# Sparse attention with an MoE block: key rows turned round, zero fills dropped, and the whole issue order rewritten

## The chip, the cores and the metric

The kernel runs on one core of a Trainium2 chip. The metric is the device time of one launch in microseconds (us); the median of three runs before the change is 217.11 us (216.6 to 217.87). The engines are named as in the profile: PE (TensorE matmuls), PEld (its weight loads), DVE (VectorE), ACT (ScalarE), POOL (GpSimd, which here issues all loads) and SP (SyncE, which issues the stores and some moves inside the chip).

## The reference

Four batches, eight heads, 768 positions, head size 64. Each query attends to the keys less than 16 positions away and, beside them, to 24 summaries of blocks of 32 positions; the result of the eight heads goes through two dense layers.

```python
k_sum = k.reshape(B, H, nb, 32, D).max(axis=3)
v_sum = v.reshape(B, H, nb, 32, D).mean(axis=3)
scores_l = where(abs(i - j) < 16, q @ k.T / 8, -1e9)
scores_s = q @ k_sum.T / 8 + log(32)
a = softmax(concat([scores_l, scores_s]))
x = a @ concat([v, v_sum])             # (4*768, 512) after the heads are joined
h = x @ w_in                           # 512 -> 2048
g = h * clip(h + 3, 0, 6) / 6
out = g @ w_out                        # 2048 -> 512
```

Inputs and output are float32; the kernel computes in bf16 and accumulates in float32.

## The kernel before

Queries are cut into 12 tiles of 64 a head. For each tile the stationary operand of the score matmul is a group of 120 key rows out of 128 in `kaug`: 32 rows of the tile before, the tile's own 64 rows, and the 24 block maxima. The queries are shifted by 16 positions (`PAD`), so that a query tile's window lies within these 96 rows. `vaug` holds the values in the same three groups of partitions: 0:32 from the tile before (the "halo", tokens `h`), 32:96 own, 96:120 the block sums (tokens `u` and their spreading). The scores of a half batch go to the "S" PSUM buffers (two of them), ACT takes exponentials (`exp`, L521), DVE multiplies with a 0/1 mask (`masking`, L522), and PE multiplies with `vaug` (tokens `v`). DVE takes the reciprocal and scales (L606), and the result is transposed into `x`, by PE for batches 0 and 1 and by DVE and SP for batches 2 and 3.

The dense part runs over eight half batches (`s` 0 to 7) of 384 rows. First layer: tokens `F{s}x{ft}`, 16 of them a half batch, each four matmuls of 128x128 by 384 columns into one of **three** "h" PSUM banks (L667); then ACT makes `relu` (L671) and DVE the product (`gate`, L672), which frees the bank. Second layer: tokens `G{s}{ts}x0`, parts 0 to 3 of four matmuls each with 512 columns into the one "o" bank (L684), a copy to SBUF (part 4) and a store (part 5); the last group is cut into 256 and 128 columns. So a first-layer group can start only when the product of the third group before it is done.

Batch 0 is special: its queries and keys are loaded in another layout and transposed on PE (`k0` to `k3`, `q0` to `q3`), its attention is taken apart (tokens `v00` to `v03`, the own part and the summed part as separate matmuls, `values1a` and `values1b`). For the later batches DVE transposes keys (`turn`, L456) and for batches 2 and 3 queries too (L460), tokens `w{b}{p}`, one for each pair of heads.

Nothing is scheduled by a compiler. The string `ORDER` lists about a thousand tokens, and each engine issues its own in that order and waits on semaphores for its inputs; `:A` and `:D` choose ACT or DVE for a copy that either can do. Tokens that begin with `-`, `~`, `_` or `=` are fills: matmuls on constant data (`keep`, L778) that only keep PE busy, of 128, 512 and 64 columns each, and `=n` one of 64n columns. POOL's loads are in the same string: `K`, `Q`, `V` for the inputs, `I` for w_in, `O` for w_out.

Of the kernel before, what the change touches and what calls it, by code (L numbers as in the profile page):

```python
# [9 lines left out]
F32 = mybir.dt.float32  # L10
BF16 = mybir.dt.bfloat16
# [18 lines left out]
c.0 K00.0 c.7 c.17 c.6 c.8:A K01.0 c.10:D c.5 c.1 _40 -15 k0.0 k0.2:A c.18 ~1 =2 k1.0 K02.0 ~12 =3 k2.0 k3.0 c.15:D c.2 c.3  # L30
s000.0 k0.3:A c.13:D c.4 c.11:A k1.1 Q00.0 q0.0 k1.4 k0.1 c.20 k1.2:A Q01.0 ~2 =5 q1.0 k0.4 k1.3:D c.9:A c.14:A c.19 k2.3:A
q0.1:A s000.1 q0.2:A =1 s010.0 s010.1 k2.2:A k3.2:D k3.3:D k3.1 V00.0 h000.0:D h001.0:D k2.1 k2.4 s000.2 ~2 =5 v00.0 V01.0 u0.0
h010.0:D s020.0 c.16 s010.2 q1.2:A u0.3:D u0.1:D u0.4:D v01.0 v01.1 v01.2 v00.1 q1.1:A V02.0 h020.0:A h021.0:A h011.0:A v00.2
s020.1 v01.3 v00.3 V03.0 u1.0 u1.3:A h030.0:D s030.0 k3.4 ~2 s030.1 u1.4:D v01.4 h031.0:D Q0w0.0 Q0w1.0 v01.5:D Q0w2.0 =1 q3.0
q3.1:D q2.0 u1.1:A u1.2:D s020.2 v02.0 v02.1 v02.2 s021.0 v02.3 s030.2 v03.0 v03.1 q2.1:A v03.2 s011.0 v03.3 v00.4 v00.5:D
v02.4 s021.1 s011.1 s021.2 v03.4 v03.5:D s011.2 v02.5:A s031.0 s031.1 s001.0 s031.2 I2.0 F0x3.0 F0x3.1 F0x3.2 F0x3.3 F0x3.4
F0x3.5 I4.0 F0x6.0 F0x6.1 F0x6.2 F0x4.0 F0x4.1 F0x4.2 F0x4.3 v411.0 v411.1 F0x5.0 F0x4.4 F0x4.5 v411.2 s001.1 I8.0 u0.2:A
s001.2 F0x8.0 F0x8.1 F0x8.2 F0x5.1 I0.0 F0x5.2 F0x11.0 F0x1.0 F0x11.1 F0x11.2 F0x1.1 F0x1.2 F0x1.3 F0x1.4 F0x1.5 v410.0 v410.1
F0x7.0 F0x7.1 F0x7.2 v410.2 F0x10.0 F0x10.1 I12.0 F0x13.0 F0x13.1 F0x15.0 F0x15.1 F0x13.2 F0x10.2 v411.3 v411.4:D v410.3
v410.4:A F0x15.2 F0x14.0 F0x14.1 F0x14.2 F0x9.0 F0x9.1 F0x9.2 F0x0.0 F0x0.1 F0x2.0 F0x2.1 K13.0 K10.0 c.12:A F0x0.2 K12.0 K11.0  # L40
w10.0 Q1w1.0 F1x14.0 F1x14.1 F1x14.2 F1x4.0 F1x4.1 F1x4.2 F1x2.0 F1x2.1 F1x2.2 w10.1:D F0x2.2 F0x2.3 F0x2.4 F0x12.0 F0x12.1
F0x12.2 F1x8.0 F1x8.1 F1x8.2 F1x1.0 F1x1.1 F1x1.2 F0x0.3 F0x0.4 F0x0.5 F0x2.5 F1x9.0 F1x9.1 F1x9.2 F1x5.0 F1x5.1 F1x5.2 F1x15.0
F1x15.1 w11.0 w11.2 F1x15.2 w11.3:D Q1w4.0 Q1w2.0 Q1w0.0 w10.2 w10.3:D q6.0 q6.1:A q7.0 q7.1:A F1x7.0 F1x7.1 w11.1:A F1x7.2
F1x12.0 F1x12.1 F1x12.2 O0.0 G02x0.0 Q1w5.0 Q1w3.0 q4.0 q4.1:A q5.0 q5.1:A F1x6.0 F1x6.1 F1x6.2 O1.0 G02x0.1 s100.0 s100.1
s100.3 F1x3.0 w12.0 F1x11.0 F1x11.1 w13.0 w13.2 F1x3.1 F1x11.2 w12.2 w12.1:D O2.0 G02x0.2 s101.0 s101.1 O3.0 F1x10.0 G02x0.3
G02x0.4:A w13.3:D w13.1:A s101.3 F1x0.0 G00x0.0 G00x0.1 w12.3:D s100.2 s101.2 s100.4 V10.0 h100.0:D F1x10.1 h110.0:A F1x10.2
F1x3.2 s110.0 s110.1 s110.2 s101.4 s110.3 G00x0.2 G00x0.3 G00x0.4:A V12.0 u4.0 h130.0:D h120.0:A F1x0.1 u4.1:D u4.2:A u4.4:D
u4.3:D u4.5:D G02x0.5 G01x0.0 G01x0.1 G01x0.2 s110.4 F1x0.2 h111.0:A v100.0 v100.1 v100.2 h121.0:A v101.0 v101.1 v101.2 G01x0.3
G01x0.4:A K20.0 K21.0 K22.0 K30.0 K23.0 w21.0 F1x13.0 F1x13.1 F1x13.2 v100.3 v100.4:A w20.0 w21.3 G12x0.0 w21.2:A v101.3
# [54 lines left out]
class Plan:  # L104
# [29 lines left out]
    def issue(self, keep):  # L134
# [28 lines left out]
def kernel(  # L163
# [80 lines left out]
    def low(x):  # L244

        return (1 - x) * HQ
# [563 lines left out]
```

## Time and profile before

| | before |
|---|---|
| median of the runs | 217.11 us |
| span of the profiled execution | 214.9 us |
| PE busy | 208.8 us, 97% |
| DVE busy | 162.7 us, 76% |
| ACT busy | 135.9 us, 63% |
| POOL busy | 49.5 us, 23% |
| first matmul of the first layer | 24.17 us |
| start of the last copy, after the last matmul | 211.96 us |

The span is the profiled execution from its first to its last instruction; the runs' times hold 2.2 us more around it. Times in the views count from the span's start. "Busy" counts overlapping instructions of an engine once. The digits of part 2 of the page are busy tenths in 40 slices of 5.4 us. In a timeline a line is start, duration, engine, line of the code, operation, and in square brackets the idle time before it and what ended it.

### The profile page before, as it was taken

How to read it: one execution, taken by the hardware profiler on the slowest of the kernel's cores; microseconds unless marked ns; L12 is line 12 of the kernel's file. 1: busy time of each engine (PE TensorE's matmuls, PEld its weight loads, DVE VectorE, ACT ScalarE, POOL GpSimd, SP SyncE). 2: the span in 40 equal slices, each digit the busy share in tenths (PEclk: the TensorE clock that was granted, in tenths of full speed). 3: DMA queues.
4: the chain of work that ended last, by engine and by line, in shares of the span. 5: the costliest groups of instructions: out<-in, count | busy, mean ns of one | idle time of the engine just before them, and what ended most of it. 6: DMA issues, size and time to landing. Idle time of an engine off the chain costs nothing.

```text
span 214.9 us, 6125 instructions
## 1 busy us (share of the span) xinstructions
PE 208.8 (97%) x2564; PEld 119.7 (56%) x2564; DVE 162.7 (76%) x318; ACT 135.9 (63%) x264; POOL 49.5 (23%) x66
## 2 busy tenths in 40 slices
PE   7998999999999999999999999999999999999994
PEld 7566656555555565565555555555555555564443
DVE  6987999999899999898899889887865555550021
ACT  3987878887898988756578696566346355520110
POOL 7977358906643244000000000000000000000000
PEclk9999999999999999999999999999999999999999
DMA  5999999999999999930334234113314400113123
GB/s 75 159 155 189 203 188 170 190 203 162 206 160 187 181 135 151 108 146 11 38 37 143 28 37 110 49 21 39 70 19 81 78 0 3 49 49 122 52 80 139
DMA packets 91724, 22.68 MB, mean 106 GB/s; under 512 B 82224, under 2 KB 88752, under 8 KB 91696
## 3 DMA queue, kind: packets, MB, share of 16 engines
q0 software_dynamic: 62288, 14.41, 72.7%
q1 hardware_dynamic: 29264, 7.80, 15.4%
q8 instruction: 20, 0.33, 0.6%
q10 hardware_dynamic: 144, 0.07, 0.1%
q14 instruction: 8, 0.07, 0.1%
HBM read 28.82 MB, written 6.29 MB: 163 GB/s over the span
## 4 chain that ended last, share of the span: by engine, by line
PE 86%; POOL 5%; DMA 4%; DVE 1%; ACT 1%; issue 1%; POOLq 0%
PE h L667 38%; PE o L684 33%; PE h L684 5%; DMA qwide<-in_q_dram 4%; PE S L624 3%; PE S L513 3%; POOL vaug L344 2%; PE S L554 1%; ACT vaug L242 1%; POOL first L306 1%; PE S L637 1%; POOL qwide L326 1%; PE S L440 1%; PE S L667 1%; POOL first L313 1%; PE h L582 1%
## 5 line engine op out<-in xcount | busy, mean ns | idle before, releaser
L667 PE MATMUL h<-x,win 128*128 128x384 bf16 x500 | 91.1, 326 | 0.3 <-DVE g L672 0.3
L671 ACT ACTIVATE r<-h 128x384 f32<-128x384 f32 x125 | 58.7, 492 | 38.8 <-PE h L667 36.8
L672 DVE SCALAR_TENSOR_TENSOR g<-r,h 128x384 bf16<-128x384 f32 x125 | 65.7, 546 | 22.7 <-ACT r L671 20.1
L684 PE MATMUL o<-wout,g 128*128 128x512 bf16 x336 | 81.7, 379 | 0.0
L667 PEld LDWEIGHTS <-win 128*128 128x128 bf16 x512 | 48.7, 98 | 35.9 <-issue 0.5
L684 PEld LDWEIGHTS <-g 128*128 128x128 bf16 x416 | 38.7, 98 | 37.4 <-issue 0.3
L521 ACT ACTIVATE at<-S 120x768 bf16<-120x768 f32 x24 | 18.6, 811 | 5.5 <-PE S L513 5.4
L242 ACT COPY ot<-o 128x512 f32<-128x512 f32 x17 | 10.0, 586 | 15.4 <-PE o L684 14.2
L522 DVE TENSOR_TENSOR at<-at,mask 96x768 bf16<-96x768 bf16 x24 | 12.6, 549 | 2.0 <-ACT at L521 1.6
L606 DVE TENSOR_TENSOR xn<-S,rc 128x768 bf16<-128x768 f32 x14 | 13.3, 950 | 0.3
L242 DVE COPY ot<-h 128x512 f32<-128x512 f32 (+1 forms) x3 | 1.6, 555 | 14.3 <-PE h L684 14.3
L344 POOL DMA_DIRECT2D vaug<-in_v_dram x10 | 11.8, 1191 | 0.4 <-DMA first<-in_k_dram 0.2
L684 PE MATMUL h<-wout,g 128*128 128x128 bf16 (+2 forms) x80 | 11.4, 294 | 0.0
L468 DVE TENSOR_REDUCE red<-kaug 128x24 bf16<-128x768 bf16 x12 | 11.2, 942 | 0.1
L242 ACT COPY vaug<-vaug 32x640 bf16<-32x640 bf16 (+3 forms) x17 | 8.9, 574 | 0.8 <-DMA vaug<-in_v_dram 0.5
L242 ACT COPY vaug<-vs 24x1536 bf16<-24x1536 bf16 x6 | 8.8, 1468 | 0.6 <-DVE vs L242 0.5
L456 DVE STREAM_TRANSPOSE kaug<-kraw 128x768 bf16<-128x768 bf16 x8 | 8.1, 1020 | 0.3 <-PE S L513 0.3
L778 PE MATMUL o<-idle 128*128 128x64 bf16 (+2 forms) x70 | 7.0, 278 | 1.1 <-DVE idle L288 1.1
L334 POOL DMA_DIRECT2D kraw<-in_k_dram x8 | 5.9, 737 | 8.9 <-DVE kaug L456 7.3
L513 PEld LDWEIGHTS <-kaug 32*128 32x128 bf16 x576 | 5.3, 92 | 4.4 <-issue 3.6
L643 DVE STREAM_TRANSPOSE y<-xn 128x768 bf16<-128x768 bf16 x8 | 7.6, 964 | 0.2
L624 PEld LDWEIGHTS <-at 120*64 120x64 bf16 x336 | 6.2, 111 | 2.6 <-issue 1.5
(107 smaller groups left out, 183.6 us busy)
## 6 DMA issues: line engine op xcount, KB each, us to landing
out_dram<-ot SPq DMA_DIRECT2D x19, 256.0 KB, 2.3
vaug<-in_v_dram POOLq DMA_DIRECT2D x6, 384.0 KB, 13.1
wout<-in_moe_w_out_dram POOLq DMA_DIRECT2D x4, 512.0 KB, 9.9
win<-in_moe_w_in_dram POOLq DMA_DIRECT2D x3, 512.0 KB, 10.8
kraw<-in_k_dram POOLq DMA_DIRECT2D x8, 192.0 KB, 12.9
x<-y SPq DMA_DIRECT2D x64, 24.0 KB, 2.0
first<-in_k_dram POOLq DMA_DIRECT2D x6, 192.0 KB, 12.3
first<-in_q_dram POOLq DMA_DIRECT2D x6, 192.0 KB, 12.3
```

Of the source, the lines that this page charges most:

```text
L242: {"ACT": nc.scalar.copy, "DVE": nc.vector.tensor_copy, "POOL": nc.gpsimd.tensor_copy}[eng](o, i)
L344: op("POOL", "dma128", lambda: nc.gpsimd.dma_start(out=o[BLK:WIN, a:z, 0:D], in_=rows[:, a:z]), w=[("v", b % 2, c) for c in range(lo, hi)] ...
L468: op("DVE", "max", lambda: nc.vector.tensor_reduce(red.slot[:], w[:, :, BLK:WIN].rearrange("p t (n c) -> p t n c", n=2), axis=AX.X, op=ALU ...
L513: nc.tensor.matmul(X[g // 2].slot[:, g % 2, i * QB:(i + 1) * QB], kaug[2 * u + m][rows, t], qT[rows, 2 * u + m, t * QB:(t + 1) * QB], star ...
L521: op("ACT", "exp", lambda a=a, e=e: nc.scalar.activation(a, X[e].slot[0:KEYS, :, 0:HALF], AF.Exp, scale=scl), r=[X[e]], w=[("at", p, half)])
L522: op("DVE", "masking", lambda m=m: nc.vector.tensor_tensor(m, m, mask[:, low(half):low(half) + HQ].unsqueeze(1).to_broadcast([WIN, 2, HQ, ...
L606: nc.vector.tensor_tensor(o, src[..., 0:D], r.unsqueeze(len(r.shape)).to_broadcast(list(o.shape)), op=ALU.mult)
L624: nc.tensor.matmul(X.slot[64 * c:64 * c + 64, i, m:m + D + 1], a[:, t * QB:(t + 1) * QB], vaug[b % 2][0:KEYS, h, t, 0:D + 1], start=True, ...
L667: nc.tensor.matmul(bank(h)[:, 0:HALF], w_in_sb[:, kt, cols], xt[s].slot[:, kt], start=(kt == 0), stop=(kt == NP - 1))
L671: op("ACT", "relu", lambda: nc.scalar.activation(r.slot[:], bank(h)[:, 0:HALF], AF.Relu, bias=0.5, scale=1.0 / 6.0), r=[h], w=[r])
L672: op("DVE", "gate", lambda: nc.vector.scalar_tensor_tensor(gt[s].slot[:, ft], r.slot[:], 1.0, bank(h)[:, 0:HALF], op0=ALU.min, op1=ALU.mul ...
L684: nc.tensor.matmul(o.slot[:, a:z], gt[s].slot[:, ft, ts * 128:(ts + 1) * 128], w_out_sb[:, ft, a:z], start=(ft == 0), stop=(ft == NFT - 1))
```

## The change

- **Key rows.** A tile's group becomes its own 64 rows first and the next 32 rows behind them; the 16 positions of shift lie at the other side. `qT`, `kaug`, `vaug`, the mask, the halo copies, the loads and the stores follow; half 0 of a batch is now tiles 0 to 5 and no longer 6 to 11.
- **No zero fills.** The block sums of v (`sums2`, `sums4`) read the own 64 rows alone, at partitions 0:64, and so need neither zeros in the halo rows (`empty`, eight operations, five on ACT and three on DVE) nor wait for them; a halo copy no longer waits until the sums are taken.
- **Block sums by 128 queries.** For batch 0, `values1b` multiplies two query tiles at once: 6 matmuls for a pair of heads and no longer 12.
- **Fills.** `idle` becomes a bf16 view of a float32 tile of ones, and a new fill token `^n` issues n products of float32 by float32 with 512 columns. The fills before: `_40 -15 ~1 =2 ~12 =3 ~2 =5 =1 ~2 =5 ~2 =1`. After: `_36 -16 ^3 ~2 ^1 =6 ~1 =3`.
- **Order.** The string is new throughout. The loads of batch 0 and of w_in keep their places in POOL's order (but for the three `Q0w`); behind them the loads are permuted. Some copies change engine.

```diff
-c.0 K00.0 c.7 c.17 c.6 c.8:A K01.0 c.10:D c.5 c.1 _40 -15 k0.0 k0.2:A c.18 ~1 =2 k1.0 K02.0 ~12 =3 k2.0 k3.0 c.15:D c.2 c.3
+c.0 K00.0 c.11 K01.0 c.1 c.7 c.8 K02.0 _36 -16 k1.0 c.2 c.3 c.6 k1.1 k0.0 k1.4 c.10 c.9 Q00.0 c.5 Q01.0 V00.0 ^3 ~2 q0.0 k2.0
...
+v03.1 v03.2 v01.5:A ~1 =3 q3.0 v03.3 q2.0 Q1w4.0 q3.1:D v00.4 s021.0 u1.2:D v00.5:D q2.1:A v02.4 v02.5:D s031.0 v03.4 s021.1
+F0x3.0 u1.4:D F0x3.1 s031.1 v03.5:D F0x3.2 s011.0 s031.2 F0x3.3 s001.0 F0x6.0 s011.1 s021.2 F0x4.0 F0x4.1 F0x3.4 s011.2 F0x3.5
...
+s100.0 K20.0 F1x12.2 F1x10.1 s100.3 F1x10.2 w12.0 s100.1 G02x0.2 F1x5.0 w13.2 G02x0.3 w13.1:D w12.1:A s101.0 G02x0.4:A s101.3
+F1x0.0 w12.2 K31.0 G00x0.0 G00x0.1 s101.1 w13.3:A w12.3:D s110.0 V22.0 G00x0.2 G00x0.3 F1x5.1 F1x13.1 Q32.0 s110.1 F1x5.2
+s100.2 s101.2 s100.4 s110.3 s110.2 K30.0 h130.0:D u4.0 G00x0.4:A Q22.0 F1x13.2 G01x0.0 F1x0.1 G01x0.1 s110.4 u4.1:D G01x0.2
...
+G32x0.1 v211.2 w31.4:A G32x0.2 F4x9.2 u6.2:A v211.3 v210.3 G32x0.3 F4x2.1 v211.4 F4x2.2 G32x0.4:A w33.0 F4x14.0 u6.4:D G11x0.5
+F4x13.0 F4x14.1 v211.5 F4x13.1 F4x7.0 v211.6 w30.4:A G30x0.0 F4x14.2 F4x7.1 F4x13.2 G30x0.1 F4x7.2 w32.3 F4x6.0 w32.4:A w33.3
...
-G70x0.4:D G70x0.5 G60x0.0 G60x0.1 G60x0.2 G72x0.4:D G72x0.5 G60x0.3 G71x256.1 G71x256.2 G60x0.4:D G60x0.5 G71x256.3 G71x256.4
-G71x384.0 G71x384.1 G71x384.2 G71x384.3 G71x384.4:D G71x384.5
+G60x0.4:A G72x0.3 G70x0.1 G71x0.4:D G50x0.5 G71x384.0 G61x0.5 G71x384.1 G71x384.2 G72x0.4:A G70x0.2 G71x256.0 G71x384.3 G70x0.3
+G71x0.5 G71x256.1 G70x0.4:A G72x0.5 G71x256.2 G71x384.4:D G60x0.5 G71x384.5 G71x256.3 G71x256.4 G70x0.5
...
-    ind = sb([WIN, NQ, 32], BF16, "ind")
+    ind = sb([QB, NQ, 32], BF16, "ind")
-    idle = sb([128, 128], BF16, "idle")
+    ones = sb([128, 128], F32, "ones")
+    idle = ones[:].bitcast(BF16)[:, 0:128]
...
     def low(x):
-        return (1 - x) * HQ
+        return x * HQ
...
-    def empty(eng, i, c):
-        o = vaug[i][0:BLK, 2 * c:2 * c + 2, :, 0:D].bitcast(F32)
-        if eng == "DVE":
-            nc.vector.memset(o, 0.0)
-        else:
-            nc.scalar.activation(o, idle[0:BLK, 0:1].unsqueeze(1).unsqueeze(1).to_broadcast([BLK, 2, NQ, D // 2]), AF.Copy, scale=0.0)
...
-        op("POOL", "dma128", lambda: nc.gpsimd.dma_start(out=o[BLK:WIN, a:z, 0:D], in_=rows[:, a:z]),
+        op("POOL", "dma128", lambda: nc.gpsimd.dma_start(out=o[0:QB, a:z, 0:D], in_=rows[:, a:z]),
...
+        def summed():
+            for T in range(3):
+                for h in range(2):
+                    nc.tensor.matmul(bank(X)[:, part(T, h)], at[p][WIN:KEYS, h, 2 * T * QB:(2 * T + 2) * QB], vf[p][WIN:KEYS, h, 0:D + 1],
+                                     start=False, stop=T == 2 and h == 1)
...
     def keep(n, m, o):
-        n, c = (1, n) if m == 3 else (n, (2, 8, 1)[m])
+        n, c = (1, n) if m == 3 else (n, (2, 8, 1, 0, 8)[m])
+        w = ones[:] if m == 4 else idle
         for _ in range(n):
-            nc.tensor.matmul(o[:, 0:c * 64].rearrange("p (c x) -> p c x", c=c), idle[:], idle[:, 0:64].unsqueeze(1).to_broadcast([128, c, 64]),
+            nc.tensor.matmul(o[:, 0:c * 64].rearrange("p (c x) -> p c x", c=c), w, w[:, 0:64].unsqueeze(1).to_broadcast([128, c, 64]),
                              start=True, stop=True)
```

211 lines of the change are left out of this document (100 added, 111 removed).

## The prediction

> **What bounds the kernel now.** I read the page first, whose digits by slice ask for the busy time by stage, then who PE waited for, then PE's timeline at the start.
>
> ```profile
> 24.17:58.30 34.13, 33.81 (x511) 19.63 (x506) 31.68 (x61) 27.99 (x52) 20.05 (x23) 1.00 1.75 187
> 58.30:123.90 65.60, 65.50 (x848) 36.66 (x849) 60.56 (x105) 50.59 (x99) 10.66 (x12) 1.00 1.12 111
> 123.90:211.95 88.05, 88.02 (x765) 48.18 (x763) 50.47 (x92) 39.31 (x81) 0.00 (x0) 1.00 0.24 56
> 211.95:214.90 2.95, 0.00 (x0) 0.00 (x0) 0.29 (x1) 0.00 (x0) 0.00 (x0) 1.00 0.39 133
> sum 214.90, PE 208.84 PEld 119.68 DVE 162.67 ACT 135.95 POOL 49.46; mean PE 41.77 PEld 23.94 DVE 32.53 ACT 27.19 POOL 9.89
> ```
>
> A row is a stretch, its length, then the busy time of PE, PEld, DVE, ACT and POOL, the granted clock (1.00), DMA. PE is busy 208.8 of 214.9 us and without a gap from 24.17 on, so the time is PE's work plus what it spends on fills and waits. DVE's total, 162.7, is 76%, but that is a mean: from 58.3 to 123.9, which is from the block sums of batch 1 (`u4.0`) to the middle of F4, it has 60.56 of 65.60, 92%, and behind that 57%.
>
> ```profile
> PE h L667 <- DVE g L672: 0.3, 1, 0.3
> ```
> ```profile
> 1.13 3.71 PE L778 MATMUL o<-idle 128*128 128x64 bf16 x55 [1.13 <-DVE idle L288]
> ...
> 5.99 0.53 PE L392 MATMUL h<-ident,first 96*64 96x96 bf16 x16 [0.26 <-DMA first<-in_k_dram]
> 6.45 2.85 PE L778 MATMUL o<-idle 128*128 128x512 bf16 x13
> ...
> 20.31 0.73 PE L442 MATMUL h<-ident,qwide 128*128 128x128 bf16 x10 [0.81 <-DMA qwide<-in_q_dram]
> ...
> 21.28 0.38 PE L582 MATMUL h<-vf,at 24*64 24x65 bf16 x12
> 21.59 0.35 PE L490 MATMUL S<-qT,kaug 64*128 64x64 bf16 x12
> ...
> 24.17 2.12 PE L667 MATMUL h<-x,win 128*128 128x384 bf16 x12
> ```
>
> Of the first 24 us about nine are fills; the stage's last wait ends when the last piece of q lands, just ahead of 20.31. From 24.17, where the first layer starts, to 211.96, where the last copy starts, PE waits only once, 0.3 us for a gate on DVE. So a gain must come from an earlier 24.17, and everything behind it must keep pace with PE; DVE, with 5 us to spare in the stretch of 65.6, is the one to watch.
>
> **The change part by part.** *The start.* The loads up to w_in keep their places, so the last q still lands at 20.3 (three loads of the same bytes only change places). What changes is how much is behind that landing. Before, the matmuls, reciprocals and scales of v02 and v03 came after it; now they come before it. From the landing I count for the new order: q3 and q2 0.73 (21.04), v00's transpose 0.2, then s021 waits for the copy of q3, which stands on DVE behind v03's scale (a copy 0.56, so about 21.6), two score groups at 0.31 (21.28 to 21.59 is one group of twelve), and two transposes at 0.2: first layer at 22.7 in place of 24.17, a gain of 1.47. Without any wait it is 22.2; with DVE half a us later, 23.2. But two score groups that stood before 24.17 (s011, s001) now stand behind: 0.62 back. Against that, PE changes from small matmuls to F or G 26 times behind this point and no longer 28 times, at 0.11 each (below): 0.2. Sum -1.47 + 0.62 - 0.2 = **-1.05**, with ends -0.5 and -1.5.
>
> *Zero fills, sums by 128 queries, fills by float32.* Six matmuls less for each of four pairs are 4 x 0.15 = 0.6 us of PE, but all stand ahead of 20.3, where PE waits 0.81 for q now: nothing, and -0.6 if q came earlier. The eight zero fills stand almost all ahead of the first keys' landing (the matmul at 5.99 waits for DMA): nothing. The three float32 products stand between the first two key groups (the second ends at about 6.9) and the first q, which POOL issues at 4.75 and which lands 5.2 later, at 9.9:
>
> ```profile
> first<-in_q_dram POOLq DMA_DIRECT2D x1, 192.0 KB, 5.2
> ```
>
> They have 3 us. No row shows a float32 product: a bf16 one of 512 columns is 0.22 (thirteen in 2.85, the last one short); if each operand is worked on as two halves it is four times that, 0.87, and three with two bf16 ones take 3.0. I take 0.87; from 0.22 to 0.87 they cost nothing, and if the clock is low in them too (the row of 55 fills makes 4480 columns in 3.71 us, half the rate of the thirteen) they take 5.1 and end near 12.5, 2.6 us late for q, of which PE's slack ahead of 20.3 (0.7 us, counted on its work from q to the landing) and a fill behind them leave some 1.5. The Trainium skill, FP8 and Floating Point Precision, section TensorE Precision Notes, says that true float32 takes four passes. By that rule the three take 2.6 us, as above; no run here shows it yet.
>
> *The order in the middle.* F4x7 takes the bank that F4x2's gate frees. Take PE from the end of `u4.0` to F4x7's start in the new order, and DVE from `u4.1` to F4x2's gate, which is all that it must do by then. The prices are from these rows:
>
> ```profile
> 55.19 0.48 PE S L513 x48
> ...
> 57.50 0.84 PE S L554 x48
> ...
> 61.09 0.95 PE S L624 x48
> 62.03 0.97 PE o L684 x4
> ...
> 65.19 1.73 PE o L684 x8
> 66.91 1.30 PE h L667 x8
> ```
> ```profile
> 28.92 1.48 DVE L672 SCALAR_TENSOR_TENSOR g<-r,h 128x384 bf16<-128x384 f32 x3
> ```
> ```profile
> L606 DVE TENSOR_TENSOR xn<-S,rc 128x768 bf16<-128x768 f32 x14 | 13.3, 950 | 0.3
> L522 DVE TENSOR_TENSOR at<-at,mask 96x768 bf16<-96x768 bf16 x24 | 12.6, 549 | 2.0 <-ACT at L521 1.6
> L468 DVE TENSOR_REDUCE red<-kaug 128x24 bf16<-128x768 bf16 x12 | 11.2, 942 | 0.1
> L456 DVE STREAM_TRANSPOSE kaug<-kraw 128x768 bf16<-128x768 bf16 x8 | 8.1, 1020 | 0.3 <-PE S L513 0.3
> L643 DVE STREAM_TRANSPOSE y<-xn 128x768 bf16<-128x768 bf16 x8 | 7.6, 964 | 0.2
> L242 DVE COPY vaug<-vs 24x1536 bf16<-24x1536 bf16 x6 | 3.4, 573 | 0.2
> L599 DVE RECIPROCAL rc<-S 128x12 f32<-128x12 f32 x14 | 3.0, 222 | 0.2
> ```
> ```profile
> L521 ACT ACTIVATE at<-S 120x768 bf16<-120x768 f32 x24 | 18.6, 811 | 5.5 <-PE S L513 5.4
> ```
>
> PE: 37 F at 0.65 (24.05), 32 G at 0.863 (27.6), eight values at 0.47, five scores at 0.48, two sums at 0.78, four transposes at 0.34 (11.1 together), and twelve changes back to F or G at 0.11 (0.97 less 0.86): **62.1 us**. DVE: an instruction in a row costs some 0.03 less than its mean, as three gates in 1.48 and not 1.64 show. 36 gates at 0.494 (17.8), eleven masks at 0.52 (5.7), eight reciprocals and scales at 1.12 (9.0), fourteen transposes of keys and queries at 0.99 (13.8), six maxima at 0.91 (5.5), six spreads at 0.54 (3.2), four block transposes at 0.93 (3.7), and thirteen small copies, 3.5 in all: **62.2 us**. So the new order asks DVE for all of its time in this stretch. The old order has 39 F and 35 G between the same two points, 65.7 us of PE, for about the same work of DVE; the new one has two F and three G fewer there, and puts a query transpose, two halo copies, two copies of x, three small ones of q and an output copy more on DVE. And DVE does not start level. The gate of F1x5 stands behind its relu, which on ACT's order stands behind the two exponentials of s101 (0.81 each), a copy of G02 (0.56) and one of keys (0.41): 2.9 us after s101 on PE. Behind that gate are another gate, five masks and a halo copy, 3.9 with it; so `u4.1` can start 6.9 us or more after s101 ends, while PE needs 5.6 (one F, four G, s110 and the sums) to the end of `u4.0`. That is 1.3; the relu before s101's has 0.3 more in front. I take 1.6, in place of 0.1 now, with 0.8 as the low end. F4x7 then starts 1.6 + 62.2 + 0.05 - 62.1 = **1.75 us** late, and PE has waited that much by then, in steps: the same sum to F3x15 (84 instructions against 49.9 us of PE) gives 1.0. Bounds: if `u4.1` starts level, and DVE's prices are 1% lower, nothing; with every mean at its full row (0.546 a gate), it would be over 4, which the row of three gates excludes; I hold 0 to 2.6. Behind 123.9 DVE's share falls to 57%, and it falls behind no more.
>
> *Loads in the middle.* The pieces of w_in still land as before, and F now needs them a us earlier: 0.1, at most 0.4. The later loads need no more than now: the first need of each stands about where it stood, behind as many bytes.
>
> *The end.* The old order ends with a 128-column piece: a copy of 0.29, a 64 KB store.
>
> ```profile
> 211.96 0.29 DVE L242 COPY ot<-h 128x128 f32<-128x128 f32 x1 [0.82 <-PE h L684]
> ```
> ```profile
> out_dram<-ot SPq DMA_DIRECT2D x1, 64.0 KB, 1.6
> ```
> ```profile
> out_dram<-ot ACTq DMA_DIRECT2D x1, 64.0 KB, 2.1
> ```
> ```profile
> out_dram<-ot SPq DMA_DIRECT2D x19, 256.0 KB, 2.3
> ```
>
> Copy and store take 0.3 + 1.6 = 1.9, and the span ends 1.05 after. The new one ends with a 64 KB store by ACT (0.33 + 2.1) and, beside it, a whole 256 KB one whose copy ends as PE does (2.3 to 2.5): 2.4, so **+0.5** (0.3 to 0.7).
>
> Sum: -1.05 + 1.75 + 0.1 + 0.5 = +1.3 on 214.9, a span of 216.2. The median of the runs is 217.11; the 2.2 around the span stay. The 0.1 of w_in is left out, because PE waits longer for DVE later anyway: 217.11 + 1.2 = **218.3 us**.
>
> **The rivals.** *DVE keeps up.* Everything hangs on 1.6 us of start and on 1% of 62; if DVE's small copies are cheaper or the exponentials of s101 come sooner, the middle costs nothing: -1.05 + 0.1 + 0.5 = -0.45, **216.6**, no change that shows. For it: the old order left PE one wait. Against it: 92% became 100%. It isn't slower, and it decides once `u4.1` starts within 0.1 us of `u4.0`'s end. *The start gives all and the end costs nothing:* -1.5 at the start, middle and end nothing: **215.6**. The copy of 256 KB would have to land in 2.0. *The fills cost:* PE is left idle from the end of the 52 fills (4352 columns, to about 4.7) until the second key piece, the one that the matmul at 5.99 waits for, and the float32 products run at the low rate: 1.5 later, **219.5** or more. The Trainium skill, TensorE: Matmul & The Clock Gate, section What's actually happening, has the clock fall only after an idle window of about 3.4 us, so not by these 1.3 us; the longest idle time here, 0.81, shows no fall, and no run shows 1.3.
>
> **How the numbers follow.** A measurement here can't tell under 0.5%, 1.09 us, from no change: faster is below 216.0, slower above 218.2. My forecast has 0.55 and, with its spread of 0.6, lies above 218.2 in 0.35 and between in 0.20. DVE keeps up: 0.27, of which 0.17 between and 0.10 below. The full gain: 0.08, below. The fills: 0.10, above. Faster 0.18, same 0.37, slower 0.45. The range reaches from the full gain to the fills, 215.8 to 219.5; the forecast's own is 217.5 to 219.1.
>
> **What would show it.** The first F matmul at 22.2 to 23.2, with the last q landing at 20.3. PE waiting for DVE's gates (L667 behind g L672) and for scales between 75 and 130 us, together 1 to 2.5 us, and DVE at 98% or more of 60 to 120. The float32 fills at 0.87 each, ending before 10 us. 3.4 us or more from the last matmul's end to the span's end. I am wrong if PE's waits behind 45 us stay under 0.5 us, or if the first F comes after 23.5.

## The result, and the profile after

The changed kernel takes 220.0 us (median of 219.11 to 221.57) against 216.86 (216.36 to 217.87): a ratio of 1.015, 95% interval 1.0101 to 1.0199. It is slower by 1.5%; 218.3 was predicted, and at most 219.5. Here and below the ratio and its interval leave out executions that are more than 1.5% above the fastest of the same kernel, and the medians count all. The profiled execution has a span of 217.8 us against 214.9; its own time is 219.55.

First the busy time by stage, cut where the prediction cut it (PE, PEld, DVE, ACT, POOL, granted clock, DMA).

```profile
24.69:58.30 33.61, 32.68 (x478) 19.33 (x481) 30.72 (x59) 27.09 (x56) 17.99 (x23) 1.00 1.79 183
58.30:123.90 65.60, 64.05 (x878) 36.21 (x886) 62.71 (x112) 47.11 (x96) 12.52 (x13) 1.00 1.06 104
123.90:213.95 90.05, 89.21 (x763) 49.09 (x773) 49.34 (x96) 40.74 (x80) 0.00 (x0) 1.00 0.27 62
213.95:217.80 3.85, 0.22 (x4) 0.04 (x1) 0.00 (x0) 0.44 (x2) 0.00 (x0) 0.92 0.29 101
```

The first F (the first matmul of the first layer) comes at 24.69 in place of 24.17, from there to the start of the last matmul it takes 189.26 in place of 187.53, and the end from there 3.81 in place of 3.18: +0.5, +1.7 and +0.6. DVE's work from 58.3 to 123.9 is 62.71 of 65.60 us, 96%, where it was 60.56.

PE's timeline of the start, and then DVE's:

```profile
6.33 0.87 PE L383 MATMUL h<-ident,first 96*64 96x96 bf16 x32 [1.39 <-DMA first<-in_k_dram]
7.13 3.27 PE L775 MATMUL o<-ones 128*128 128x512 f32 x8
...
15.90 0.83 PE L527 MATMUL h<-vaug,ind 64*32 64x128 bf16 x23 [1.04 <-DMA vaug<-in_v_dram]
...
23.68 0.35 PE L481 MATMUL S<-qT,kaug 64*128 64x64 bf16 x12 [0.76 <-DVE qT L242]
...
24.69 0.65 PE L663 MATMUL h<-x,win 128*128 128x384 bf16 x3
```
```profile
12.74 0.96 DVE L394 TENSOR_REDUCE red<-h 128x24 bf16<-128x768 bf16 x1 [1.41 <-ACT kaug L242]
...
22.60 0.56 DVE L602 TENSOR_TENSOR xn<-h,rc 128x384 bf16<-128x384 f32 x1
23.08 0.55 DVE L242 COPY qT<-S 128x768 bf16<-128x768 bf16 x1
```

The last piece of q landed at 20.13, and yet the copy of q3, which I had ending at 21.6, starts at 23.08 and ends at 23.63. DVE has no idle time from 12.74 on: 10.3 us of its work stand between the third pair's maximum (`k2.1`) and that copy. The last idle time ahead of them is the 1.41 us in which the maximum waits for ACT's copy out of the same PSUM bank (`k2.3`).

Behind the first F, PE's waits, the moves on SP and ACT at the end:

```profile
PE o L680 <- issue: 1.2, 4, 0.7
...
PE h L663 <- DMA x<-y: 0.7, 1, 0.7
```
```profile
102.21 11.09 SPq L645 DMA_DIRECT2D x<-y  x16
```
```profile
214.86 0.27 ACT L694 COPY ot<-h 128x128 f32<-128x128 f32 x1 [0.74 <-DMA out_dram<-ot]
215.16 0.37 ACTq L695 DMA_DIRECT2D out_dram<-ot  x1
```

PE never waits for a gate. It waits 0.7 us at 57 for nothing that the profile shows ("issue"), 0.7 at 116 for the sixteen moves of x to F4 (0.69 us each to issue), and the last piece waits for an output buffer, that is for an older store to land. In the second profile of this kernel (`e18`) nothing shows at 57, the same F4 group waits 0.93 us at 117, which the profile puts down to DVE, and the last piece does not wait; from the first F to the end both take 193.1 us.

### The profile page after: what moved, and what is told of

The parts are those of the page before. It is cut to its first block, busy times and chain, and to the rows that moved or that the text cites. A ratio compares the mean times of both kernels' runs of the same rounds, so it can differ in the third digit from the quotient of the medians.

```text
span 217.8 us, 6018 instructions
## 1 busy us (share of the span) xinstructions
PE 206.1 (95%) x2498; PEld 119.1 (55%) x2525; DVE 159.5 (73%) x316; ACT 129.5 (59%) x257; POOL 49.4 (23%) x66
## 4 chain that ended last, share of the span: by engine, by line
PE 76%; DVE 6%; DMA 6%; SPq 4%; issue 3%; POOL 1%; ACT 1%; DVEq 0%; ACTq 0%; POOLq 0%
PE h L663 36%; PE o L680 29%; SPq L645 4%; PE h L680 3%; DMA first<-in_q_dram 3%; PE S L504 2%; DVE vaug L242 2%; PE S L620 2%; DMA out_dram<-ot 2%; DMA x<-y 1%; POOL first L296 1%; PE S L633 1%; PE S L663 1%; DVE red L394 1%; DVE xn L602 1%
## 5 line engine op out<-in xcount | busy, mean ns | idle before, releaser
L663 PE MATMUL h<-x,win 128*128 128x384 bf16 x500 | 93.3, 326 | 0.7 <-DMA x<-y 0.7
L667 ACT ACTIVATE r<-h 128x384 f32<-128x384 f32 x125 | 59.6, 492 | 44.2 <-PE h L663 43.1
L680 PE MATMUL o<-wout,g 128*128 128x512 bf16 x311 | 78.6, 379 | 2.4 <-issue 1.2
L335 POOL DMA_DIRECT2D vaug<-in_v_dram x10 | 12.2, 1229 | 13.0 <-DVE rc L595 11.5
L513 DVE TENSOR_TENSOR at<-at,mask 96x768 bf16<-96x768 bf16 x24 | 12.7, 546 | 1.9 <-ACT at L512 1.9
L459 DVE TENSOR_REDUCE red<-kaug 128x24 bf16<-128x768 bf16 x12 | 11.1, 934 | 0.0
L242 ACT COPY kaug<-h 128x576 bf16<-128x576 bf16 (+3 forms) x12 | 4.1, 413 | 7.2 <-DVE red L394 7.0
L775 PE MATMUL o<-ones 128*128 128x64 bf16 (+3 forms) x60 | 7.1, 302 | 1.1 <-DVE ones L280 1.1
L242 DVE COPY ot<-h 128x256 f32<-128x256 f32 (+1 forms) x2 | 0.7, 358 | 10.0 <-PE h L680 10.0
L242 ACT COPY vaug<-vs 24x1536 bf16<-24x1536 bf16 x5 | 7.3, 1468 | 0.2
## 6 DMA issues: line engine op xcount, KB each, us to landing
wout<-in_moe_w_out_dram POOLq DMA_DIRECT2D x4, 512.0 KB, 10.3
kraw<-in_k_dram POOLq DMA_DIRECT2D x8, 192.0 KB, 10.4
first<-in_k_dram POOLq DMA_DIRECT2D x6, 192.0 KB, 13.5
first<-in_q_dram POOLq DMA_DIRECT2D x6, 192.0 KB, 10.3
```

The source lines that it names most:

```text
L242: {"ACT": nc.scalar.copy, "DVE": nc.vector.tensor_copy, "POOL": nc.gpsimd.tensor_copy}[eng](o, i)
L335: op("POOL", "dma128", lambda: nc.gpsimd.dma_start(out=o[0:QB, a:z, 0:D], in_=rows[:, a:z]), w=[("v", b % 2, c) for c in range(lo, hi)], s ...
L459: op("DVE", "max", lambda: nc.vector.tensor_reduce(red.slot[:], w[:, :, 0:QB].rearrange("p t (n c) -> p t n c", n=2), axis=AX.X, op=ALU.ma ...
L513: op("DVE", "masking", lambda m=m: nc.vector.tensor_tensor(m, m, mask[:, low(half):low(half) + HQ].unsqueeze(1).to_broadcast([WIN, 2, HQ, ...
L663: nc.tensor.matmul(bank(h)[:, 0:HALF], w_in_sb[:, kt, cols], xt[s].slot[:, kt], start=(kt == 0), stop=(kt == NP - 1))
L667: op("ACT", "relu", lambda: nc.scalar.activation(r.slot[:], bank(h)[:, 0:HALF], AF.Relu, bias=0.5, scale=1.0 / 6.0), r=[h], w=[r])
```

## The experiments

Ratios are to the kernel before, timed on the same chip. All kernels but the twelfth and the fifteenth are made from the changed one.

### Is it the order or the layout?

**Old order, new layout** (`e1`):

```diff
-(the new ORDER)
+(the ORDER of before: no empty(), load pieces renamed)
```


> The changed kernel with the order of before: its layout, its dropped zero fills, its block sums over 128 queries, but the old order and the old bf16 fills. If the new order is what costs (my theory: about 0.9 us at the start, 1.4 in the middle, 0.65 at the end), this one is as fast as before or a little faster: ratio 0.995 to 1.001, first F matmul at 23.9 to 24.2, no wait of PE above 0.5 us behind it. If the layout costs (rows of v in partitions 0 to 63 land later, as the trace of after shows 1.2 to 1.9 us later than before), V00 lands at about 14.4 here too, the first F is at 24.7 or later and the ratio is 1.003 to 1.008.

217.53 us, ratio 1.0019 (0.9996 to 1.0042), just above what I expected. The layout, the dropped zero fills and the sums over 128 queries together cost 0.4 us, between nothing and 0.9; the order, with its fills, costs the rest of the 1.5%. From the first F to the end it takes 190.5 us, as before (190.7). But in its profile the first F comes at 25.47, and 24.7 or later was my sign that the layout costs. DVE's last idle time there is a wait for a piece of v:

```profile
14.82 1.01 DVE L242 COPY vaug<-vaug 32x768 bf16<-32x768 bf16 x3 [1.54 <-DMA vaug<-in_v_dram]
```

In the two profiles of before that wait is 0.67 and 0.86 us. So a part of what the start loses, up to 0.9 us, can be the layout's.

**Its counterpart** (`e9`): the old order up to the first F, the new one behind.

```diff
-c.0 K00.0 c.11 ... v03.4 s021.1 | F0x3.0 u1.4:D ...    (new | new)
+c.0 K00.0 c.7  ... s001.0 s031.2 | F0x3.0 F0x3.1 ...   (old | new)
```


> The counterpart of the fifth experiment: the changed kernel with the old order up to the first F matmul (as in the first experiment) and the new order behind it. If start and rest add up as the two traces of before and after say (rest 193.1 us from the first F to the end, less 0.6 for the two score groups that now stand ahead, against 190.5 with the old rest), this kernel takes 1.5 to 2 us more than the first experiment: 218.9 to 219.6, ratio 1.010 to 1.014. If the start alone carries the loss (fifth experiment: new start and old rest give 1.0158, as slow as after), it is as fast as the first: 1.001 to 1.004.

219.76, ratio 1.0119 (1.0078 to 1.016): over `e1` the new rest costs 1.0%. In its profile it takes 193.2 us, as in the changed kernel (193.1).

**New start, old rest** (`e5`), and the same join later (`e6` ahead of `u6.0`, `e7` ahead of `F6x8.0`).

```diff
-... v03.4 s021.1 | F0x3.0 u1.4:D ...                   (new | new)
+... v03.4 s021.1 | h011.0:A u1.4:D s011.0 ... F0x3.0 F0x3.1   (new | old)
```


> The changed kernel with the new order only up to the token ahead of the first F matmul, and from there the tokens in the order of before (so s011 and s001 stand ahead of the first F again). If the new start is worth nothing and what follows costs 1.4 us in the middle and 0.5 at the end (my reading of the two traces), this kernel is near before: ratio 1.000 to 1.005, and no wait of PE over 0.5 us behind the first F. If the start itself carries the loss (a first F that comes late, or a granted clock that falls because PE waits early), the ratio stays at 1.010 or more and the clock of several runs is 0.992 or lower.

220.14, ratio 1.0158 (1.0124 to 1.0192), against my 1.005. The rest takes 190.2, as in the old order, but the first F comes at 28.15. Part of that is made by the join, which puts score groups back to back on two S buffers:

```profile
PE S L481 <- ACT at L487: 1.4, 1, 1.4
```

Without those 1.4 us the new start costs some 0.7% over the old one in `e1`. That is an estimate from one profile, in which the full rate of the matmuls also came late (at 9.8 us; the clock, below). With it 0.7% + 1.0% is about what the whole loses over `e1`, 1.3% here and 1.6% in `e18`. That the rest loses is shown by `e9`; that the start does is not, since the profiles of the old start on the new layout have their first F at 25.47 (`e1`), 25.83 (`e9`) and 24.66 (`e14`), and those of the changed kernel's start, with no join or fall of the clock ahead of it, at 24.2 to 25.9.

> The same with the cut ahead of the block sums of batch 2 (u6.0, at about 116 us): new order for the start and the first part of the middle, old order behind. My reading: against the previous kernel it adds the waits at 57 and 64 us, some 0.6 to 0.9 us with the scores that stand behind the first F; ratio 1.005 to 1.009. If DVE's saturation costs as in the prediction (1.6 us late at u4.0, paid by F4x7), it adds 1.5 or more: ratio 1.009 to 1.013.

> The same with the cut ahead of F6x8.0 (at about 155 us): only the last quarter in the old order. My reading: against the previous kernel it adds the wait for the moves of the first blocks to F4 (0.8 us at 116 us), and lacks the end's 0.5: ratio 1.010 to 1.013, last matmul to end 3.2 us. If the end is the larger part, the ratio is 1.005 to 1.008.

1.0343 (1.03 to 1.0386) and 1.0365 (1.0323 to 1.0408): both far slower than either order whole. The joins made waits of their own, of which these are the rows of `e6` and then of `e7`:

```profile
PE S L620 <- DVE vs L242: 3.0, 1, 3.0
```
```profile
PE h L663 <- DVE g L668: 2.7, 2, 2.4
```

They tell nothing on the middle; they suggest that where copies stand in DVE's queue is worth more than what they take.

**Before once more** (`e12`), the same code, for where v lands.

> The kernel before once more, for a second profile of its start. If the rows of v land late in the changed kernel because of their new partitions (V00 13.5 to 15.0, V03 17.7 to 19.0 in ten profiles with the new layout, 13.2 and 16.5 in the one profile with the old), V03 lands below 17.2 here too. If landings only vary from run to run, it may lie anywhere up to 19.

V03 lands at 17.12 (16.49 in the first profile, 16.94 in `e15`); in the seventeen profiles with rows of v in partitions 0 to 63 it lands at 17.25 to 19.02. It is later by about 1.3 us in the mean; by `e1` that costs 0.9 us at most. The first F comes at 24.14.

### What makes the start late?

**The third maximum ahead of ACT's copy** (`e3`).

```diff
-... q0.1:A k2.3:A V02.0 ... c.4 k2.1 s000.1 ... q1.2:D s030.0 h000.0:D s000.2 ...
+... q0.1:A V02.0 ... c.4 k2.1 k2.2:D s000.1 ... q1.2:D s030.0 h000.0:D s000.2 k2.3:A ...
```


> The changed kernel with the maximum and the first copy of the third pair's keys (k2.1, k2.2 on DVE) ahead of the copy of the same bank by ACT (k2.3), which now stands behind the exponential s000.2. My theory: two readers of one bank on different engines take turns in the order written, DVE's 1.41 us of idle time at 11.3 goes, k2.1 starts at 11.5 to 11.7, and as DVE has no other gap up to the first F it starts 0.7 to 1.2 us earlier, 23.5 to 24.0; ratio to before 1.008 to 1.012. Rival: DVE would only wait later, for the rows of v (landing 14.4 to 18.4) or for the last q (20.1), and the first F gains under 0.3 us: ratio 1.013 to 1.016.

220.60, ratio 1.0165 (1.0116 to 1.0213): no gain. In its profile the maximum waits for no copy any more, but its own transposes are late, because the fills in front of them ran at half rate. The rows are stretches again; the eighth number is the granted clock:

```profile
4.00:7.42 3.42, 1.78 (x42) 1.41 (x41) 1.33 (x4) 0.00 (x0) 3.28 (x8) 1.00 1.08 159
7.42:10.83 3.41, 3.41 (x5) 1.35 (x4) 3.13 (x14) 1.75 (x5) 3.41 (x5) 0.50 1.46 165
```

**The same, with the transposes ahead of the first q, fewer fills ahead of them, and three fills in the first idle time; behind the start, the mends of `e10`** (`e11`).

```diff
-_36 -16 k1.0 ... ^3 ~2 q0.0 k2.0
+_36 -16 ~3 k1.0 ... ^2 ~1 k2.0 q0.0
```


> The previous kernel and, at the start, the third pair's keys as in the third experiment (maximum and first copy on DVE ahead of ACT's copy), with their transposes ahead of the first q, fewer fills in front of them (two float32 products and one of bf16 in place of three and two) and three more fills behind the first ones. In six profiles of this order the first F came 11.8 to 11.95 us after that maximum started on DVE (12.5 to 13.9). If that chain on DVE sets the start, the maximum now starts at 11.2 to 11.5 and the first F at 23.0 to 23.4, and the time is 1.0 to 1.5 below the previous kernel: ratio 1.000 to 1.005. If the rows of v or the last q are next, the first F stays at 24 or later and the ratio within 0.3% of the previous kernel's.

The maximum starts at 11.60, as soon as DVE is free, and the first F 12.2 us later:

```profile
11.60 0.95 DVE L394 TENSOR_REDUCE red<-h 128x24 bf16<-128x768 bf16 x1
...
23.84 0.65 PE L663 MATMUL h<-x,win 128*128 128x384 bf16 x3
```

That is the earliest first F of all kernels with the new start, 0.85 us ahead of the changed kernel's, and not the 23.0 to 23.4 expected: two waits of 0.2 to 0.3 us came up on the way. The wait for ACT's copy is thus one part of the late start; DVE's own work behind the maximum is the larger one. The time, 220.59 (ratio 1.0172, 1.0146 to 1.0199), is spoilt by the mends behind (below) and by 1.3 us of "issue".

**bf16 in place of float32 fills** (`e2`).

```diff
-^3 ... ^1
+~12 ... ~4
```


> The changed kernel with its four float32 fill products replaced by sixteen bf16 ones of the same length (twelve for three, four for one). My theory: nothing but their number changes; time within 0.3% of after (ratio to before 1.012 to 1.018), landings of K01, K02, Q00 as in after (6.3, 9.3, 10.6). Rival: the float32 products disturb the loads or the clock; then K02 and Q00 land 0.4 to 0.7 us earlier here, as in before, and the first F is 0.4 or more earlier (ratio 1.008 to 1.012).

220.49, ratio 1.0165 (1.012 to 1.021): float32 does no harm that shows. One float32 product takes 0.86 us (two records of 0.43 in the changed kernel, at 8.10, 8.52 and 8.95), four times a bf16 one of 0.215.

### The clock

Most executions of the kernels with the new start were granted a mean clock of 0.97 to 0.992 (`e11` and `e17` apart), most of the kernel before 0.998 to 1.000. The traces of the falls show whole stretches of 3.41 us at half rate, on a fixed grid.

**Fills in PE's three early idle times** (`e8`).

```diff
-_36 -16 k1.0 ... ^1 =6 u0.0 ... q2.0 Q1w4.0
+_36 -16 ~5 k1.0 ... ^1 =6 ~4 u0.0 ... q2.0 ~3 Q1w4.0
```


> The changed kernel with bf16 fills of 512 columns put into its three early idle times of PE: five behind the first fills (1.39 us idle before the first keys' second piece), four ahead of the first block sums (1.04 us), three behind the last query transpose (0.76 us). If those idle times make the granted clock fall in some executions (0.976 to 0.992 in most runs of after and of the kernels made from it, in whole steps of 3.4 us at half rate in the trace of the third experiment), the clock is 0.998 or more in nearly all runs, the median goes from 220.0 to about 219.2 and the slowest runs below 220; ratio 1.010 to 1.013. If the clock has nothing to do with these idle times, it varies as before and the ratio stays at 1.015 or rises by what the fills take.

221.04, ratio 1.0197 (1.0163 to 1.0231), slower, and the clock 0.992 or less in all six: my reason fell. The fall comes behind a stretch in which PE was busy for 3.02 of 3.42 us:

```profile
14.10:17.51 3.41, 3.41 (x49) 1.72 (x47) 3.29 (x9) 2.84 (x6) 2.00 (x3) 1.00 2.64 152
17.51:20.93 3.42, 3.02 (x97) 2.51 (x93) 3.17 (x10) 3.26 (x6) 2.98 (x6) 1.00 1.56 195
20.93:24.34 3.41, 3.41 (x39) 2.61 (x36) 2.97 (x9) 0.96 (x4) 2.33 (x3) 0.50 1.25 205
```

But its matmuls are small: `64*32`, `24*128`, `96*64` and `64*128` rows and columns of the array, where a fill uses `128*128`. So I counted, from the records of eighteen profiles, each grid stretch's use of the array: streamed columns (2400 a us) times rows/128 times columns/128.

```
use of the array    stretches    clock at half in the next
under 0.30               5             5
0.30 to 0.35            13             8
0.35 and over         1079             2
```

The bounds were drawn from the same cases that they sort; a use 0.8% lower would make it 6 of 7, 7 of 12 and 2. Of the fifteen stretches with half rate behind them, five were at half rate themselves, which halves their use. The other ten come ahead of the falls from the full rate. Four of these falls follow a stretch in which PE was idle for about half of the time or more (busy for 0.53 to 1.78 of 3.42 us, in `e3`, `e6`, `e7` and `e14`), six a stretch in which it was busy for 2.3 to 3.2 us with small matmuls. In the start the lowest stretch of the changed kernel's two profiles lies at 0.39 and 0.32, in kernels with the same start at 0.18 to 0.39, in the two profiles of before at 0.40 and 0.38.

**Fills inside that stage** (`e17`), and **the changed kernel again** beside it (`e18`, no edit).

```diff
-_36 -16 k1.0 ... s030.1 u1.0 ... v00.1 ... v01.4
+_36 -16 ~3 k1.0 ... s030.1 ~1 u1.0 ~1 ... v00.1 ~1 ... v01.4 ~1
```


> The changed kernel with seven bf16 fills of 512 columns on the whole array: three behind the first fills, and one each behind s030's scores, the second block sums, v00's summed part and v01's transposes, that is inside 17 to 21 us, where PE looks busy but with matmuls that use 24 to 96 rows and 32 to 64 columns of the array. In 1097 stretches of 3.41 us of eighteen profiles the clock fell to half behind all five whose matmuls, weighted by the rows and columns in use, came to less than 0.30 of the full array's, behind 8 of 13 from 0.30 to 0.35, and behind 2 of 1079 above; in the changed kernel those around 17 to 21 us lie at 0.27 to 0.39. If that weighted use decides, the clock is now 0.998 or more in at least five of six runs and the median is 219.0 to 219.6, against 219.9 to 220.5 for the changed kernel itself in the next run. If it doesn't, the clock is 0.992 or less in most runs as in the eighth experiment, and the median is no lower than the changed kernel's.

> The changed kernel itself once more on the same chip, as the measure for the previous run: median 219.9 to 220.5, clock 0.992 or less in at least half of the runs; ratio 1.012 to 1.019.

With the fills 219.24 us (218.83 to 219.88), ratio 1.0112 (1.0085 to 1.0139), and the clock 1.000 in all six; without them 220.57 (220.37 to 221.74), ratio 1.0178 (1.015 to 1.0206), clock 0.982 to 0.998. Seven more matmuls make the kernel 1.3 us faster. Which of the seven does how much was not tried apart. The four inside the stage are likely what ended the falls, since `e8` filled the idle times alone and its clock fell in all six; but `e11`, without them and at 0.32 of the array, was granted 0.998 to 1.000 in four of five. Part of the gain is at the very start. First PE's rows of the changed kernel again, then the kernel with fills:

```profile
6.01 1.49 PE L383 MATMUL h<-ident,first 96*64 96x96 bf16 x32 [1.07 <-DMA first<-in_k_dram]
7.43 4.49 PE L775 MATMUL o<-ones 128*128 128x512 f32 x8
```
```profile
5.58 0.63 PE L775 MATMUL o<-ones 128*128 128x512 bf16 x1
6.16 1.00 PE L383 MATMUL h<-ident,first 96*64 96x96 bf16 x32
7.09 3.27 PE L775 MATMUL o<-ones 128*128 128x512 f32 x8
```

Both have their grid at the same place (3.06 and 3.09, 6.48 and 6.50, 9.89 and 9.91). With the idle time filled, matmuls run at the full rate from 6.48 on; without, from 9.91 on (the float32 records stand 0.85 apart until 9.3 and 0.43 from 10.04), so that the third maximum starts at 13.99 and not at 12.51. The granted clock of the views reads 1.00 all the while: the trace's clock records begin only where the full rate does, at 9.91 and at 6.48, and the views count the time ahead of the first record as full. Where the grid lies differs from one execution to the next, and the changed kernel's start goes with it:

```
profile                    full rate from   third maximum   first F
e4                               4.8            12.50        24.28
e6                               4.9            12.48        24.23
changed kernel                   5.6            12.74        24.69
e17 (idle time filled)           6.5            12.51        24.31
e2                               9.3            13.68        25.59
e7                               9.9            13.91        25.66
e18 (changed kernel again)       9.9            13.99        25.88
```

The first F follows the maximum by 11.7 to 12.0 us in all seven: DVE's chain is what sets it. In `e5` (9.8), `e10` (9.4) and `e13` (12.7) the full rate came late too, but there the join or a fall of the clock puts the first F off further.

### What costs behind the start?

**Four mends** (`e10`): h120 ahead of h110, G32 ahead of F4, the end of `e4`, six output buffers.

```diff
-h110.0:D h100.0:A h120.0:D ... F4x9.0 F4x8.0 ... F4x8.1 G32x0.0 ... G32x0.3
+h120.0:D h110.0:D h100.0:A ... G32x0.0 ... G32x0.1 ... G32x0.2 F4x9.0 F4x8.0 ... G32x0.3
-"ot": ... for i in range(4)
+"ot": ... for i in range(6)
```


> The changed kernel with four mends behind the start: halo copy h120 ahead of h110 on DVE, the second layer G32 ahead of the first F4 groups (so that the sixteen moves have 1.7 us more), the end's order of the fourth experiment, and six output buffers in place of four. If the waits at 64 and 116 us and the wait for an output buffer at the end are what the rest costs, from the first F to the span's end it takes 191.3 to 192.0 us in place of 193.1, and 1.0 to 1.7 us less than after in all: ratio 1.008 to 1.012. If DVE is simply full, the same waits come back at other places and it gains under 0.4.

223.40, ratio 1.0278 (1.0236 to 1.0319): worse. A part of that is the clock, 0.977 to 0.992 in all six; but from the first F to the end it takes 194.3 us, where 191.3 to 192.0 was expected. The wait for the moves is gone, and a longer one for a gate stands in its place, at 125 us here and at 123 in `e11`:

```profile
PE h L663 <- DVE g L668: 1.8, 1, 1.8
```

**Nine small copies from DVE to ACT** (`e13`).

```diff
-h110.0:D h100.0:A h120.0:D ... v101.4:D ... w21.4:D G12x0.4:D ... w20.4:D ... v110.4:D ... w20.5:D ... w21.5:D ... w22.5:D
+h120.0:A h110.0:D h100.0:A ... v101.4:A ... w21.4:A G12x0.4:A ... w20.4:A ... v110.4:A ... w20.5:A ... w21.5:A ... w22.5:A
```


> The changed kernel with nine small copies of the middle (a halo copy, two copies of x, an output copy, two spreads of maxima, three of q's edges) moved from DVE to ACT, as the old order has them: 2.8 us less for DVE from 60 to 116 us, some 4.5 more for ACT, which is busy 70% there. If DVE being full is what makes PE wait in the middle (63.9 and 116 us, and in the tenth and eleventh experiment 1.8 us for a gate at 123 to 125), those waits go and the first F to the span's end takes 0.6 to 1.0 us less than after's 193.1; ratio 1.008 to 1.012. If the moves' issue on SP sets F4's start by itself, the wait at 116 us stays at 0.5 or more, and the ratio is 1.012 or more.

222.32, ratio 1.0223 (1.0188 to 1.0257); its two executions at the full clock took 220.77 and 221.12, no less than the changed kernel. DVE is busy for 58.6 us from 58.3 to 123.9, in place of 62.7. The wait at 116 us is gone, as DVE being full would have it, but others came at 68 and 75 us, one of them for a copy that now stands on ACT:

```profile
PE S L620 <- DVE vaug L242: 0.6, 1, 0.6
PE S L504 <- ACT x L242: 0.5, 1, 0.5
```

**The reverse on the old order** (`e14`): eight such copies from ACT to DVE.

```diff
-h120.0:A ... v101.4:A ... G12x0.4:A ... w21.4:A ... w20.4:A ... v110.4:A ... w21.5:A ... w22.5:A
+h120.0:D ... v101.4:D ... G12x0.4:D ... w21.4:D ... w20.4:D ... v110.4:D ... w21.5:D ... w22.5:D
```


> The reverse: the first experiment (new layout, old order) with eight such copies moved from ACT to DVE. DVE's 92% of 60 to 125 us becomes 96%, as in after. If DVE being full is what costs in the middle, PE gets waits of 0.6 to 1.5 us in all behind 45 us, and the kernel is 0.5 to 1.5 us slower than the first experiment: ratio 1.004 to 1.009. If the order of the groups itself is what costs, it is within 0.4 us of it: ratio 1.001 to 1.004.

222.51, ratio 1.0218 (1.0184 to 1.0252), 5 us over `e1` where I expected 1.5 at most. Some of that is the clock, which fell in five of six executions, here behind the wait of 1.8 us; the one at the full clock took 220.68, 3.5 us over those of `e1`:

```profile
PE h L663 <- DVE x L242: 2.4, 2, 1.8
...
PE o L680 <- DVE ot L242: 0.5, 1, 0.5
```

So a copy put on DVE waits there behind whatever stands in front of it, and PE waits with it, although DVE is busy for only 59.2 of 65.6 us from 58.3 to 123.9 here, no more than in `e1` (60.5): it is the place in the queue that costs, and not the sum. And `e10` and `e13` don't give the time back either: taking load off, or time for the moves, in an order written for another spacing only moves the wait.

**The end** (`e4`): stores right behind their copies, G72 and G70 earlier, the 128 column piece last, by DVE.

```diff
-G71x0.4:D G50x0.5 G71x384.0 ... G70x0.3 G71x0.5 G71x256.1 G70x0.4:A G72x0.5 ... G71x256.4 G70x0.5
+G71x0.4:D G71x0.5 G70x0.0 ... G72x0.4:D G72x0.5 ... G70x0.4:A G70x0.5 ... G71x256.4 G71x384.0 ... G71x384.5
```


> The changed kernel with its last thirty tokens in another order: stores right behind their copies, the 512 column groups G72 and G70 before the last 256 columns, and the piece of 128 columns with its copy on DVE last, as in before. My theory: the end behind the last matmul shrinks from 3.85 to about 3.2 us and ACT's 0.74 us wait for a store goes: 0.5 to 0.8 us less than after, ratio to before 1.011 to 1.013. Rival: the stores are bound by their bytes (896 KB in 5.7 us at the end) and the end moves by under 0.2 us.

220.92, ratio 1.0174 (1.0122 to 1.0225): no gain. From the first F to the start of the last matmul it takes 188.7 us, 0.6 less than the changed kernel, and the end takes 4.37, 0.6 more. The last copy waits for an output buffer again:

```profile
214.45 0.29 DVE L242 COPY ot<-h 128x128 f32<-128x128 f32 x1 [4.88 <-DMA out_dram<-ot]
```

A 256 KB store issued at 210.44 in that crowd lands at 214.35, 3.9 us later. That fits the rival's reason, stores bound by their bytes, though the end grew by more than the 0.2 us that it gave.

### A faster version?

The old order lets DVE sit idle for 0.87 us ahead of the last q. **v02 ahead of that** on the kernel before (`e15`) and on `e1` (`e16`):

```diff
-Q0w2.0 =1 q3.0 q3.1:D q2.0 u1.1:A u1.2:D s020.2 v02.0 v02.1 v02.2 s021.0 v02.3 s030.2
+Q0w2.0 u1.1:A u1.2:D s020.2 v02.0 v02.1 v02.2 v02.3 s030.2 q3.0 q3.1:D q2.0 s021.0
```


> The kernel before with the values of the third pair (v02: two groups of matmuls, reciprocal, scale) ahead of the last query transposes, where DVE sat idle for 0.87 us waiting for q, and without the fill there. Here the idle time of DVE is real and on the chain to the first F: I expect the first F 0.5 to 0.8 us earlier than 24.15 and the time 0.5 to 0.8 us lower, ratio 0.9965 to 0.998. If the last landing of q and what ACT does behind it set the start, no change: 0.999 to 1.001.

> The same edit on the first experiment (new layout, no zero fills, sums over 128 queries, old order). If the layout's later landing of v (V03 1.2 us or more later) is what keeps the first experiment from being faster than before, the edit gains less here (v02 can't be ready before q): ratio 1.000 to 1.003. If not, 0.5 to 0.8 us: 0.998 to 1.000.

Both are slower: 218.32, ratio 1.0071 (1.0042 to 1.0101), and 222.66, 1.0169 (1.0139 to 1.0198). The idle time that the edit was to fill is absent in the second profile of before (`e12`), and the four executions of `e15` at the full clock took 217.38 to 217.65, no less than before. The edit also packs small matmuls together, and the clock falls. In `e15`:

```profile
19.28:22.70 3.42, 2.27 (x61) 1.84 (x61) 2.61 (x8) 1.78 (x3) 2.50 (x4) 1.00 1.26 205
22.70:26.11 3.41, 3.41 (x81) 2.80 (x75) 2.04 (x6) 2.38 (x5) 0.88 (x1) 0.50 1.31 203
```

The granted mean was 0.969 to 0.984 in all six executions of `e16`. No kernel here beats the one before.

## Why the prediction was wrong, point by point

The sign was right, and the middle and the end came out near their size. The start, on which the gain rested, came out 1.6 us worse, and the clock had no place in the sum.

**The start: -1.05 predicted, about +0.6 measured where the clock doesn't interfere** (first F at 24.31 in `e17`, 24.15 in the two profiles of before, and two score groups, 0.62, behind it, less 0.2 for switches). The failed step is "s021 waits for the copy of q3 ... so about 21.6". I counted PE from the landing of q and took DVE to be free but for one scale. The page of before gave no row for it, but the order did: `k2.3:A` stands ahead of `k2.1`, both read one bank, and 10.3 us of DVE's work follow before that copy, which ended at 23.63. `e11` shows the chain: without the wait the copy starts at 22.22 and the first F comes at 23.84, still 1.1 us behind the 22.7 of the prediction, so DVE's queue alone was priced too low. q's landing at 20.1 no longer sets the start. That loads keep their time was right for q, wrong by about 1.3 us for v, which by `e1` costs at most 0.9 us; how much of the +0.6 it is stays open.

**The clock: nothing predicted, +0.7 to 1.3 measured** (219.24 in `e17`, 220.0 and 220.57 without its fills). This is the rival "the fills cost", with its place (PE idle between the 52 fills and the second key piece, float32 products at the low rate) and nearly its price (1.5); `e18` shows it, while in the first profile of the changed kernel the full rate came at 5.6 and the price wasn't paid. The falls of the clock behind 17 us are no part of that rival; how the 0.7 to 1.3 divide between the two is open. I gave the rival 0.10, because the longest idle time of before, 0.81 us, showed no fall. The Trainium skill, TensorE: Matmul & The Clock Gate, section What's actually happening, names a free-running window of 3413 ns, and the 3.41 us grid agrees; its condition for the fall, a window of idle time, doesn't hold in `e8`, where PE was busy for 3.02 of 3.42 us.

**The middle: +1.75 predicted, about 1.4 measured, by another way.** DVE's work was counted rightly (62.7 us of 65.6) and PE does wait, but not in steps for gates. In the changed kernel PE waits for the moves (0.7), which I left out of the count though I priced their block transposes: sixteen issues in a row take 11.1 us on SP. And it waits 0.7 for nothing that the profile shows, but not in `e18`, where the stretch takes as long. That more copies on DVE cost is shown by `e14`; that DVE's load makes the 1.4 us is not, since `e13` took 2.8 us of copies off it and gained nothing. What makes it stays open, and that the size agrees is partly luck.

**The end: +0.5 predicted, +0.3 to +0.6 measured** (3.47 to 3.81 against 3.18). Right in size; the term that I didn't see is the wait of 0.74 for an output buffer, which `e18` lacks: its end is the 3.47.

**Zero fills, sums, float32 fills: 0 predicted**, and `e1` and `e2` agree; 0.86 a product was the price taken.

Sum where the clock is full: 0.6 + 1.4 + 0.4 = 2.4, and `e17` is 2.3 over before; with the clock, 3.1 to 3.7. The rivals "DVE keeps up" and "full gain" fell with the start.

**Three slips that change nothing.** In the sum for PE the "11.1 together" is 9.1 by its own prices, and the 62.1 follows from the 9.1. Fills that start at 6.9 and take 5.1 end at 12.0, not at 12.5. And the time around the span is 1.7 us and not 2.2, if span and time are of one execution (219.55 and 217.8 in the changed kernel, 217.65 and 215.9 in `e1`).

## What to carry to other kernels

Before pricing a landing or a wait that goes, follow the other engines' queues up to it: an engine that shows no idle time from some point on sets the end of the stage from the wait ahead of that point. Judge fills by how much of the array they and their neighbours use within a stretch of the clock's grid (3.41 us here), and not only by how busy PE looks; a change that packs small matmuls closer can cost more through the clock than it saves. And where two engines are over 90% busy in queues written out by hand, a copy moved or a part joined costs by its place in the queue, several times its own length.

## What the runs showed of the hardware that was not expected

- **The clock fell behind busy stretches too.** Under 0.30 of the array's full use in a stretch of 3.41 us the next one ran at half rate in 5 of 5 cases, from 0.30 to 0.35 in 8 of 13, above in 2 of 1079; in six of the ten falls from the full rate PE had been busy for 2.3 to 3.2 us. What decides between 0.30 and 0.35 is open.
- **The rate at which an execution starts isn't in the granted clock of the views.** It reads 1.00 while float32 records stand 0.85 us apart instead of 0.43, until 9.91 in `e18`, where the trace's first clock record begins.
- **PE waits for nothing that shows at much the same counts.** Seven profiles with the new rest have one wait of 0.3 to 1.3 us that no semaphore explains, each behind 1725 to 1731 of PE's records (matmuls, weight loads and its few semaphores), just in or behind a group of 48 score matmuls issued in half a us; in `e16` it is behind 1473, in `e12` behind 961, about 256 and 768 earlier, and `e4`, `e6` and `e15` have one about 1024 earlier. One of 0.33 us in `e14`, behind 2646, and two under 0.3 us in `e4` and `e8` do not fit, and `e3`, `e10`, `e13` and `e18` have no such wait. The Trainium skill, Runtime: NRT & Kernel Launch, section Instruction fetch mechanics, says that instructions are fetched in blocks of 256 and that crossing a block is mostly hidden; most of the counts above agree with the blocks. That the fetch is the cause, and so was not hidden here, is argued, not shown.
